# One written order for the stages of all units, with u and g loaded as rows and the weight casts spread over three engines

## The chip, the cores and the metric

The kernel runs on 1 core of one Trainium2 chip. The metric is the device time of one execution in microseconds, the lower the better; one launch of the kernel does the whole computation once.

## What is computed

Two layers follow each other. The first is a linear attention with a decaying state (4 batches, 8 heads, 768 steps, head size 48):

```
for t in range(S):
    cur = einsum('bhd,bhe->bhde', u * k[t], v[t])
    y[t] = einsum('bhd,bhde->bhe', r[t], state + cur)
    state = w[t][..., None] * state + einsum('bhd,bhe->bhde', k[t], v[t])
```

Its output, as 3072 tokens of 384 numbers, goes through a layer of 1024 hidden units whose activation is `h * softmax(h)`, then normalised and scaled by g:

```
h = x @ w_in
solu = h * softmax(h)
ln = (solu - mean(solu)) / sqrt(var(solu) + 1e-6) * g_ln
out = ln @ w_out
```

## The kernel before

The 768 steps are cut into 6 chunks of 128, and a unit is one chunk of one batch: 24 units, batch running fastest, so that units 0 to 3 are the first chunks of the four batches and have no state yet, and units 20 to 23 are the last ones and leave none. For each unit four inputs (w, k, r, v) of 128 x 384 float32 are loaded in 192-byte pieces. The stages of a unit, with the names used below and in the change:

- `lw` (ACT): logarithm of w. `cum` (PE): its running sums forward, two matmuls into one PSUM tile. `exp` (ACT): their exponentials in place. `kp`, `rp` (DVE): k and r times these.
- `vb`, `p`, `q` (POOL): v in bf16; r times k; that times u. `dg` (DVE): the sum of q per head. `dv` (POOL): v times that sum, the term of the present step.
- `krk`, `krr` (PE): transposes of kp and rp; `kr` (DVE): their copy to SBUF. `M` (PE): scores; `m` (ACT): their copy; `sel` (POOL): the causal mask on them, in place. `Y` (PE): attend, which sums the dv term, the state's part and the masked scores times v; `y` (ACT): its copy.
- `S` (PE), `et` (ACT), `st` (DVE): the new state of the batch.
- `X` (PE), `xT` (DVE): transposes of y. `H` (PE): 24 hidden matmuls; `e` (ACT): exp; `he` (DVE): h times e. `Oa`, `Ob` (PE): the output matmuls in two halves, with the sums that the normalisation needs; `junk` (DVE), `sq` (ACT), `qm` (POOL), `lv` (ACT): the scale of each token; `o` (ACT): the scaled output, then the store.

Once per run the weights are prepared: w_in is cast to bf16 (`setup_w_in`), and w_out is multiplied by g (`gw`, eight slices), its column mean is subtracted by PE (`mean`) and the result written to `w2` (`setup_w_out`). `InOrder` makes each engine issue its instructions in the order in which the program is written, and an engine waits at the first instruction whose inputs are missing. That order is made by a loop over ticks (the end of the function): in each tick every stage is called for one unit, at a fixed distance from the tick's number, `setup_w_in` in tick 1 and `setup_w_out` in tick 3. The loads stand in SP's queue: unit 0, u (as a broadcast to 128 partitions), w_in, unit 1, w_out, g, unit 2, and so on. PSUM holds 2 buffers of two banks (tag b: cum, m and h) and 4 of one bank (tag s: all others); loads have 5 buffers each and work tiles 3.

Of the kernel before, what the change touches and what calls it, by code (L numbers as in the profile page):

```python
# [41 lines left out]
def kernel(  # L42
# [76 lines left out]
    win_f = consts.tile([128, KM, DF], F32)  # L119
    nc.sync.dma_start(out=win_f, in_=moe_w_in.rearrange("(ko ki) f -> ki ko f", ki=128))  # L120
    load(1)
    wout_f = consts.tile([128, KF, DM], F32)
    nc.sync.dma_start(out=wout_f, in_=moe_w_out.rearrange("(ko ki) d -> ki ko d", ki=128))
    g_sb = consts.tile([128, KF], F32)
    nc.sync.dma_start(out=g_sb, in_=moe_g_ln.rearrange("(ko ki) -> ki ko", ki=128))
    load(2)
# [7 lines left out]
    def setup_w_in():
        for j in range(KM):
            dve.tensor_copy(out=win_sb[:, j, :], in_=win_f[:, j, :])

    def setup_w_out():

        gr = consts.tile([128, KF], F32)  # L140
        dve.tensor_scalar(out=gr, in0=g_sb, scalar1=RDF, scalar2=None, op0=MULT)
        gw = consts.tile([128, KF, DM], BF16)
        for f in range(KF):
# [12 lines left out]
    def cumulate(i):
        L = live[i]
        lw = L["lw"]
        cum = big.tile([C, 2, 512], F32, tag="b", name="cum_ps")
# [5 lines left out]
        cum = live[i]["ex"]  # L165
        act.activation(out=cum[:, :, :DM], in_=cum[:, :, :DM], func=EXP)

    def scaled(i):
# [1 line left out]
        kp, rp = kp_t[i % NR], rp_t[i % NR]  # L170
        ex = L["ex"][:, :, :DM].rearrange("t e (h d) -> t e h d", h=H)
        dve.tensor_mul(out=kp[:, :, :D], in0=ex[:, 0], in1=L["k"])
        dve.tensor_mul(out=rp[:, :, :D], in0=ex[:, 1], in1=L["r"])
        L["kp"], L["rp"] = kp, rp

    def bonus(i):
# [1 line left out]
        vb = wk.tile([C, H, D], BF16, tag="vb", name="vb")
        pool.tensor_copy(out=vb, in_=L["v"])
        p = wk.tile([C, H, D], BF16, tag="p", name="p")  # L180
        pool.tensor_mul(out=p, in0=L["r"], in1=L["k"])
        q = wk.tile([C, H, D], BF16, tag="q", name="q")
        pool.tensor_mul(out=q, in0=p, in1=u_bc)
        dg = wk.tile([C, H], F32, tag="dg", name="dg")
        L["q"], L["dg"], L["vb"] = q, dg, vb
# [4 lines left out]

    def bonus_v(i):
# [3 lines left out]
        pool.tensor_mul(out=dv, in0=vb, in1=dg.unsqueeze(2).to_broadcast([C, H, D]))  # L195
        L["dv"] = dv

    def transposed(i):
# [1 line left out]
        kr_ps = small.tile([C, 2 * HP, C], BF16, tag="s", name="kr_ps")  # L200
        for j, t in ((0, L["kp"]), (1, L["rp"])):
            for hp in range(HP):
                pe.transpose(kr_ps[:, j * HP + hp, :], t[:, 2 * hp:2 * hp + 2, :].rearrange("t a d -> t (a d)"), ident)
        L["kr_ps"] = kr_ps
# [168 lines left out]
    def store(i):  # L373
        L = live[i]
        c, b = units[i]
        o = io.tile([C, DM], F32, tag="o", name="o")
# [1 line left out]
        nc.sync.dma_start(out=out[b * S + c * C:b * S + (c + 1) * C, :], in_=o)

    LOOK = 4  # L380
    for t in range(-2, NU + 4):
        def do(d, *stages):
            if 0 <= t + d < NU:
                for stage in stages:
                    stage(t + d)

        if t > -2 and t + LOOK < NU:
            load(t + LOOK)
        if t == 1:
            setup_w_in()  # L390
        if t == 3:
            setup_w_out()
        do(0, bonus_v, transposed, transposed_copy)
        do(-1, state, state_decay)
        do(-2, hidden_mul)
        do(-1, state_update)
        do(-3, lambda i: output(i, 0))
        do(-4, store)
        do(-1, x_transposed, x_copy)
        do(1, log_w, bonus)  # L400
        do(0, scores, scores_copy, scores_mask)
        do(1, cumulate, decays)
        do(-3, lambda i: output(i, 1), squares, sums, centre, scale)
        do(1, scaled, bonus_sum)
        do(-1, hidden, hidden_exp)
        do(0, attend, y_copy)


# [28 lines left out]
```

## Time and profile before

| what | value |
|---|---|
| median of 3 runs | 186.49 us (185.88 to 186.62) |
| the profiled execution | 187.83 us |
| its span, first to last instruction | 186.1 us |
| mean granted TensorE clock | 0.952 |
| PE busy | 151.1 us (81%) |
| DVE, ACT, POOL busy | 120.1, 113.4, 108.0 us |
| DMA | 27.28 MB, mean 147 GB/s |

Busy shares are averages over the span. The span has a start, in which loads and weights arrive, and a long regular part; the views below are taken by stretch.

### The profile page before, as it was taken

The page shows a single profiled execution, that of the slowest core. Times are in us where ns is not written, and L with a number is a line of the kernel's source. Part 1 is how long each engine was busy: PE and PEld are TensorE (multiplying, and loading weights), DVE is VectorE, ACT ScalarE, POOL GpSimd, SP SyncE. Part 2 cuts the span into 40 slices and gives each one's busy share as a digit, 9 for nine tenths or more (in the row PEclk, how much of TensorE's full clock was granted, in tenths as well). Part 3 has the DMA queues.
Part 4 walks back from the last instruction along what each step waited for, and adds up shares of the span by engine and source line. Part 5 has one row for each costly group of instructions (what it writes and reads, how often), then busy time and mean ns, then how long its engine had stood idle before and what let it go on. Part 6 is the DMA issues. An engine that isn't in the chain of part 4 may idle for free.

```text
span 186.1 us, 5430 instructions
## 1 busy us (share of the span) xinstructions
PE 151.1 (81%) x2136; PEld 117.1 (63%) x2136; DVE 120.1 (65%) x262; ACT 113.4 (61%) x237; POOL 108.0 (58%) x154
## 2 busy tenths in 40 slices
PE   0312483865999999999999999999999999999980
PEld 0100362533578778787788778787788777787750
...
PEclk9999999585589999999999999999999999999999
...
GB/s 117 260 255 246 221 196 188 166 178 201 188 33 186 138 170 158 202 164 140 196 189 220 179 218 155 166 175 170 153 154 81 48 48 17 29 42 46 42 42 86
DMA packets 105945, 27.28 MB, mean 147 GB/s; under 512 B 101312, under 2 KB 105536, under 8 KB 105920
## 3 DMA queue, kind: packets, MB, share of 16 engines
...
HBM read 22.22 MB, written 4.72 MB: 145 GB/s over the span
## 4 chain that ended last, share of the span: by engine, by line
PE 33%; ACT 29%; POOL 13%; issue 13%; DVE 6%; DMA 3%; SPq 1%; POOLq 0%; DVEq 0%
PE o_ps L34 13%; ACT m L34 9%; ACT e L34 9%; POOL m L34 7%; PE g_ps L34 5%; ACT y L34 4%; PE m_ps L34 4%; PE h_ps L34 4%; DMA u_bc<-in_u_dram 3%; ACT lv L34 3%; PE x_ps L34 2%; DVE gw L34 2%; ACT rs L34 2%; POOL qm L34 2%; DVE w L34 2%
## 5 line engine op out<-in xcount | busy, mean ns | idle before, releaser
L34 PE MATMUL o_ps<-w,he 128*128 128x385 bf16 x192 | 53.9, 331 | 4.7 <-DVE w L34 2.2
L34 PE MATMUL g_ps<-he 128*128 128x128 bf16 x192 | 42.5, 222 | 1.1 <-ACT y L34 1.1
L34 POOL TENSOR_SCALAR_AFFINE_SELECT m<-m 128x1024 bf16<-128x1024 bf16 x24 | 26.2, 1092 | 22.5 <-ACT m L34 22.5
L34 PE MATMUL h_ps<-xT,win_sb 128*128 128x128 bf16 x576 | 38.7, 227 | 0.4 <-ACT m L34 0.2
L34 ACT CAST m<-m_ps 128x1024 bf16<-128x1024 f32 x24 | 24.3, 1011 | 20.4 <-PE m_ps L34 20.4
L34 PEld LDWEIGHTS <-win_sb 128*128 128x128 bf16 x576 | 35.0, 102 | 1.7 <-DVE xT L34 1.1
L34 PEld LDWEIGHTS <-he 128*128 128x128 bf16 x384 | 26.8, 98 | 9.8 <-issue 4.3
L34 POOL TENSOR_TENSOR dv<-vb,dg 128x384 bf16<-128x384 bf16 x24 | 20.3, 847 | 21.8 <-DVE dg L34 20.2
L34 PE MATMUL o_ps<-inv_col,e 128*128 128x1 bf16 x192 | 32.2, 168 | 0.0
L34 DVE TENSOR_TENSOR he<-h_ps,e 128x1024 bf16<-128x1024 f32 x24 | 29.2, 1215 | 4.6 <-ACT e L34 4.6
L34 PEld LDWEIGHTS <-e 128*128 128x128 bf16 x192 | 18.9, 98 | 16.5 <-issue 3.2
L34 ACT ACTIVATE e<-h_ps 128x1024 bf16<-128x1024 f32 x24 | 24.2, 1009 | 4.7 <-PE h_ps L34 4.7
L34 DVE COPY kr<-kr_ps 128x1024 bf16<-128x1024 bf16 x24 | 16.6, 690 | 11.8 <-PE kr_ps L34 11.8
L34 POOL TENSOR_TENSOR p<-r_in,k_in 128x384 bf16<-128x384 f32 x24 | 24.1, 1004 | 0.0
L34 POOL TENSOR_TENSOR q<-p,u_bc 128x384 bf16<-128x384 bf16 x24 | 22.0, 917 | 3.1 <-DMA u_bc<-in_u_dram 1.3
L34 DVE SCALAR_TENSOR_TENSOR junk<-g_ps,ident 128x128 bf16<-128x128 f32 x24 | 7.0, 291 | 22.3 <-PE o_ps L34 22.3
L34 ACT ACTIVATE cum_ps<-cum_ps 128x768 f32<-128x768 f32 x24 | 19.3, 804 | 1.3 <-PE cum_ps L34 1.3
L34 DVE TENSOR_REDUCE dg<-q 128x8 f32<-128x384 bf16 x24 | 13.0, 543 | 8.8 <-POOL q L34 8.8
L34 DVE TENSOR_TENSOR kp<-cum_ps,k_in 128x384 bf16<-128x384 f32 x23 | 12.8, 557 | 8.0 <-ACT cum_ps L34 6.8
L34 POOL CAST vb<-v_in 128x384 bf16<-128x384 f32 x23 | 11.7, 510 | 10.8 <-DMA v_in<-in_v_dram 10.8
L34 ACT ACTIVATE lw<-w_in 128x384 bf16<-128x384 f32 x23 | 11.9, 518 | 9.2 <-DMA w_in<-in_w_dram 9.2
L34 PEld LDWEIGHTS <-kr 64*128 64x128 bf16 (+1 forms) x272 | 11.5, 99 | 8.6 <-DVE kr L34 5.1
...
## 6 DMA issues: line engine op xcount, KB each, us to landing
...
```

The lines of the kernel that those rows point to most:

```text
L34: made = make(*args, **kwargs)
```

## The change

The tick loop is gone. A string ORDER names every stage of every unit (`M3` is the scores of unit 3), and a loop at the end calls them in that order. Its beginning and its end:

```
lw0 cum0 vb0 p0 win1 rows ubc exp0 q0 kp0 p1 rp0 lw1 cum1 dg0 win2 win0 exp1 kp1 krk1 krk0 rp1 krr0 kr0 gw3 M0 dv0 krr1 q1 kr1 m0 dg1 M1 sel0 m1 gw0
lw2 vb1 dv1 sel1 p2 Y0 vb2 gw1 cum2 Y1 y0 gw4 X0 exp2 gw5 gw2 q2 gw6 gw7 kp2 rp2 y1 xT0 lw3 S1 krk2 krr2 kr2 S0 X1 et1 dg2 cum3 st1 exp3 dv2 xT1 M2
mean m2 mean_sb sel2 kp3 et0 H0 e0 p3 rp3 H1 Y2 lw4 q3 w2 he0 krk3 krr3 y2 Oa0 kr3 st0 e1 M3 vb3 Ob0 X2 m3 cum4 lw5 p4 dg3 exp4 dv3 S2 he1 sel3 junk0
...
e23 Ob21 junk21 sq21 Oa22 he23 qm21 lv21 o21 Ob22 junk22 sq22 qm22 Oa23 lv22 Ob23 o22 sq23 junk23 qm23 lv23 o23
```

The rest of it, cut to what matters:

```diff
-    pe, act, dve, pool = (InOrder(tc, e) for e in (nc.tensor, nc.scalar, nc.vector, nc.gpsimd))
+    pe, act, dve, pool, sp = (InOrder(tc, e) for e in (nc.tensor, nc.scalar, nc.vector, nc.gpsimd, nc.sync))
...
-    io = ctx.enter_context(tc.tile_pool(name="io", bufs=5))
-    wk = ctx.enter_context(tc.tile_pool(name="wk", bufs=3))
+    io = ctx.enter_context(tc.tile_pool(name="io", bufs=6))
+    wk = ctx.enter_context(tc.tile_pool(name="wk", bufs=5))
...
+    u_row = consts.tile([1, DM], F32)
+    sp.dma_start(out=u_row, in_=u.rearrange("(o h) d -> o (h d)", o=1))
+    g_rows = consts.tile([KF, 128], F32)
+    sp.dma_start(out=g_rows, in_=moe_g_ln.rearrange("(ko ki) -> ko ki", ki=128))
     load(0)
+    win_f = consts.tile([128, KM, DF], F32)
+    sp.dma_start(out=win_f, in_=moe_w_in.rearrange("(ko ki) f -> ki ko f", ki=128))
+    load(1)
+    wout_f = consts.tile([128, KF, DM], F32)
+    wout_v = moe_w_out.rearrange("(ko ki) d -> ki ko d", ki=128)
+    for half in range(2):
+        part = slice(half * KF // 2, (half + 1) * KF // 2)
+        sp.dma_start(out=wout_f[:, part, :], in_=wout_v[:, part, :])
+    for i in range(2, 5):
+        load(i)
...
-    NR = 3
-    lw_t = [consts.tile([C, H, 64], BF16, name=f"lw{j}") for j in range(NR)]
+    NR = 6
+    lw_t = [consts.tile([C, H, 64], BF16, name=f"lw{j}") for j in range(2 * NR)]
...
-    u_bc = consts.tile([C, H, D], F32)
-    nc.sync.dma_start(out=u_bc, in_=u.partition_broadcast(C))
...
+    def setup_rows():
+        u_ps = small.tile([C, DM], F32, tag="s", name="u_ps")
+        pe.matmul(u_ps, lhsT=ones_row, rhs=u_row, start=True, stop=True)
+        g_ps = small.tile([128, KF], F32, tag="s", name="gt_ps")
+        pe.transpose(g_ps, g_rows, ident_f)
+        live[0]["u_ps"], live[0]["g_ps"] = u_ps, g_ps
+
+    def setup_rows_copy():
+        dve.tensor_copy(out=u_bc.rearrange("t h d -> t (h d)"), in_=live[0]["u_ps"])
+        dve.tensor_scalar(out=gr, in0=live[0]["g_ps"], scalar1=RDF, scalar2=None, op0=MULT)
+
+    def setup_w_in(j):
+        copy = (act.copy, dve.tensor_copy, pool.tensor_copy)[j]
+        copy(out=win_sb[:, j, :], in_=win_f[:, j, :])
+
+    def setup_gain(f):
+        if f % 2:
+            act.activation(out=gw[:, f, :], in_=wout_f[:, f, :], func=COPY, scale=gr[:, f:f + 1])
+        else:
             dve.tensor_scalar(out=gw[:, f, :], in0=wout_f[:, f, :], scalar1=gr[:, f:f + 1], scalar2=None, op0=MULT)
...
-        dve.tensor_add(out=w2[:, :, :DM], in0=m_ps.unsqueeze(1).to_broadcast([128, KF, DM]), in1=gw)
+        live[0]["mean_ps"] = m_ps
+
+    def setup_mean_copy():
+        act.copy(out=mean_sb, in_=live[0]["mean_ps"])
+
+    def setup_w2():
+        for f in range(KF):
+            dve.tensor_add(out=w2[:, f, :DM], in0=gw[:, f, :], in1=mean_sb)
...
+        L["vb"] = wk.tile([C, H, D], BF16, tag="vb", name="vb", bufs=8)
...
+    loaded = 5
+    for word in ORDER.split():
+        if word in once:
+            once[word]()
+            continue
+        name = word.rstrip("0123456789")
+        i = int(word[len(name):])
+        if name == "lw":
+            while loaded < min(i + 5, NU):
+                load(loaded)
+                loaded += 1
+        stages[name](i)
```

u is now bf16 in SBUF. The stages themselves are as before, but for `scaled`, `bonus` and `transposed`, which are cut into single steps that ORDER can place apart, with the same instructions.

Where the instructions move, first on POOL, the start of the program. Before, from unit 0's v cast on (the mask is AFFINE_SELECT, q is p times u_bc):

```order
12 L31 CAST vb<-v_in 128x384
13 masks.py:199 AFFINE_SELECT ident<-ident 128x128
14 L34 TENSOR_TENSOR p<-r_in,k_in 128x384
15 L34 TENSOR_TENSOR q<-p,u_bc 128x384
16 L34 TENSOR_TENSOR dv<-vb,dg 128x384
17 L34 CAST vb<-v_in 128x384
18 L34 TENSOR_TENSOR p<-r_in,k_in 128x384
19 L34 TENSOR_TENSOR q<-p,u_bc 128x384
20 L34 AFFINE_SELECT m<-m 128x1024
21 L34 TENSOR_TENSOR dv<-vb,dg 128x384
22 L34 CAST vb<-v_in 128x384
```

And now, from the q of unit 0 on:

```order
17 L63 TENSOR_TENSOR q<-p,u_bc 128x384
18 L63 TENSOR_TENSOR p<-r_in,k_in 128x384
19 L63 CAST win_sb<-win_f 128x1024
20 L63 TENSOR_TENSOR dv<-vb,dg 128x384
21 L63 TENSOR_TENSOR q<-p,u_bc 128x384
22 L63 AFFINE_SELECT m<-m 128x1024
23 L63 CAST vb<-v_in 128x384
24 L63 TENSOR_TENSOR dv<-vb,dg 128x384
25 L63 AFFINE_SELECT m<-m 128x1024
26 L63 TENSOR_TENSOR p<-r_in,k_in 128x384
27 L63 CAST vb<-v_in 128x384
```

Before, the mask of unit 0 (row 20) stood behind unit 1's cast of v, and the mask of unit 1 behind unit 2's (row 22). Now the masks of both stand ahead of unit 2's first product (row 26), and the mask of unit 0 ahead of unit 1's cast; a cast of w_in has come to POOL.

On DVE, the preparation of the weights. Before, from the casts of w_in to the first `he` behind the output weights:

```order
25 L34 CAST win_sb<-win_f 128x1024 x3
...
39 L34 TENSOR_SCALAR gr<-g_sb 128x8
40 L34 TENSOR_SCALAR gw<-wout_f,gr 128x384 x8
41 L34 TENSOR_TENSOR w_145<-mean_ps,gw 128x8x384
42 L34 COPY kr<-kr_ps 128x1024
43 L34 TENSOR_TENSOR he<-h_ps,e 128x1024
```

And now, from DVE's first instruction that waits for a load:

```order
34 L60 CAST win_sb<-win_f 128x1024
35 L63 CAST u_bc<-u_ps 128x384
36 L63 TENSOR_SCALAR gr<-gt_ps 128x8
37 L63 TENSOR_TENSOR kp_147<-cum_ps,k_in 128x8x48
...
44 L63 TENSOR_SCALAR gw<-wout_f,gr 128x384 x4
45 L63 TENSOR_TENSOR kp_149<-cum_ps,k_in 128x8x48
...
53 L63 TENSOR_TENSOR rp_156<-cum_ps,r_in 128x8x48
54 L63 TENSOR_TENSOR w_192<-gw,mean_sb 128x384 x8
55 L63 TENSOR_TENSOR he<-h_ps,e 128x1024
```

One cast of w_in now stands ahead of unit 0's kp (row 37). Four of the gw (the other four are ACT's) stand ahead of unit 2's kp (row 45), where all eight stood behind unit 3's; the eight adds that make w follow unit 3's rp (row 53).

## Rows read from the trace of the kernel before

**Rows 1.** The page's slices of the span: PE's busy tenths and granted clock.

```profile
PE   0312483865999999999999999999999999999980
...
PEclk9999999585589999999999999999999999999999
```

**Rows 2.** Windows: busy us (count) by engine, granted clock, DMA share, GB/s.

```profile
31.30:38.60 7.30, 6.50 (x70) 5.06 (x71) 5.40 (x11) 3.46 (x6) 5.23 (x7) 0.54 1.09 172
38.60:46.50 7.90, 4.04 (x25) 2.05 (x23) 7.33 (x9) 1.39 (x4) 2.32 (x3) 0.72 1.05 191
46.50:55.00 8.50, 8.09 (x86) 5.79 (x87) 4.98 (x12) 3.83 (x9) 2.55 (x5) 0.66 0.88 122
...
91.00:151.00 60.00, 58.94 (x912) 46.98 (x911) 45.91 (x102) 46.38 (x101) 44.17 (x61) 1.00 0.76 156
```

**Rows 3.** PE's timeline, the start: start us, us, instruction, idle time before it.

```profile
20.78 0.50 PE L34 MATMUL y_ps<-vb,m 128*128 128x48 bf16 x8 [4.86 <-POOL m L34]
...
25.47 2.72 PE L34 MATMUL h_ps<-xT,win_sb 128*128 128x128 bf16 x24 [0.24 <-ACT m L34]
...
31.31 0.37 PE L34 MATMUL y_ps<-vb,m 128*128 128x48 bf16 x8 [2.80 <-POOL m L34]
```

**Rows 4.** POOL's timeline, the start.

```profile
17.23 0.50 POOL L34 CAST vb<-v_in 128x384 bf16<-128x384 f32 x1 [4.98 <-DMA v_in<-in_v_dram]
...
20.69 1.26 POOL L34 TENSOR_TENSOR dv<-vb,dg 128x384 bf16<-128x384 bf16 x1
27.76 0.50 POOL L34 CAST vb<-v_in 128x384 bf16<-128x384 f32 x1 [5.81 <-DMA v_in<-in_v_dram]
```

**Rows 5.** DVE's timeline, the start: the weights.

```profile
20.18 2.92 DVE L34 CAST win_sb<-win_f 128x1024 bf16<-128x1024 f32 x3
...
37.56 4.97 DVE L34 TENSOR_SCALAR gw<-wout_f,gr 128x384 bf16<-128x384 f32 x8
43.10 3.36 DVE L34 TENSOR_TENSOR w<-mean_ps,gw 128x3072 bf16<-128x3072 f32 x1 [0.57 <-PE mean_ps L34]
```

**Rows 6.** PE's timeline, one steady unit.

```profile
90.84 0.32 PE L34 MATMUL o_ps<-w,he 128*128 128x385 bf16 x1
...
92.16 0.40 PE L34 MATMUL m_ps<-kr 64*128 64x128 bf16 x8
...
92.82 0.33 PE L34 MATMUL o_ps<-w,he 128*128 128x385 bf16 x1
...
93.81 1.50 PE L34 MATMUL h_ps<-xT,win_sb 128*128 128x128 bf16 x24
95.14 0.33 PE L34 MATMUL y_ps<-dv,ident 128*128 128x384 bf16 x1
...
95.68 0.38 PE L34 MATMUL kr_ps<-ident,kp 128*128 128x128 bf16 x4
...
96.12 0.33 PE L34 MATMUL s_ps<-st,ident 128*128 128x384 bf16 x1
...
96.83 0.32 PE L34 MATMUL o_ps<-w,he 128*128 128x385 bf16 x1
```

**Rows 7.** The page's groups: line, engine, instruction, count; busy us, mean ns.

```profile
L34 POOL TENSOR_SCALAR_AFFINE_SELECT m<-m 128x1024 bf16<-128x1024 bf16 x24 | 26.2, 1092 | 22.5 <-ACT m L34 22.5
...
L34 ACT CAST m<-m_ps 128x1024 bf16<-128x1024 f32 x24 | 24.3, 1011 | 20.4 <-PE m_ps L34 20.4
...
L34 POOL TENSOR_TENSOR dv<-vb,dg 128x384 bf16<-128x384 bf16 x24 | 20.3, 847 | 21.8 <-DVE dg L34 20.2
...
L34 DVE TENSOR_TENSOR he<-h_ps,e 128x1024 bf16<-128x1024 f32 x24 | 29.2, 1215 | 4.6 <-ACT e L34 4.6
...
L34 DVE COPY kr<-kr_ps 128x1024 bf16<-128x1024 bf16 x24 | 16.6, 690 | 11.8 <-PE kr_ps L34 11.8
...
L34 DVE TENSOR_TENSOR kp<-cum_ps,k_in 128x384 bf16<-128x384 f32 x23 | 12.8, 557 | 8.0 <-ACT cum_ps L34 6.8
```

**Rows 8.** PE's timeline, its last matmul.

```profile
180.92 0.17 PE L34 MATMUL o_ps<-inv_col,e 128*128 128x1 bf16 x1
```

More of the change, by code (lines that the diff above doesn't have):

```diff
@@ new lines @@
+dg5 sel4 qm1 H3 krr5 Oa2 kr5 lw7 e3 lv1 q6 cum6 Y4 vb6 he3 exp6 dv5 y4 p7 q7 o1 kp6 Ob2 M5 X4 rp6 junk2 m5 krk6 sq2 qm2 cum7 lw8 krr6 S3 xT4 kr6 exp7
+H4 sel5 dg6 et3 Oa3 p8 q8 vb7 lv2 st3 Y5 e4 kp7 o2 y5 rp7 Ob3 M6 S4 he4 dv6 sq3 X5 cum8 junk3 m6 S5 et4 xT5 qm3 sel6 st4 lv3 krk7 et5 H5 krr7 exp8 o3
+p9 Y6 st5 q9 Oa4 kp8 y6 lw10 e5 krk8 kr7 X6 rp8 krr8 xT6 M7 kr8 vb9 Ob4 m7 he5 sq4 dg7 sel7 lw9 S6 dv7 vb8 dg9 junk4 M8 m8 p10 qm4 H6 et6 cum9 st6 e6
+Y7 y7 exp9 Oa5 X7 dg8 Ob5 he6 xT7 kp9 q10 junk5 lv4 sel8 o4 rp9 dv8 lw11 sq5 H7 krk9 qm5 krr9 e7 kr9 lv5 dv9 Oa6 he7 o5 p11 M9 m9 Ob6 cum10 junk6 sel9
@@ new lines @@
+Y8 cum11 p12 dg10 Y9 exp10 kp10 sq6 y8 qm6 y9 X8 lv6 exp11 rp10 krk10 krr10 xT8 o6 kr10 kp11 S9 S7 vb11 rp11 et9 et7 H8 lw12 Oa7 st7 p13 M10 q13 Ob7
+st9 X9 e8 vb12 krk11 he8 m10 vb10 lw13 cum12 xT9 krr11 q11 sq7 S8 dg11 et8 dv10 kr11 H9 sel10 p14 vb13 junk7 st8 lw14 exp12 Oa8 Y10 e9 Ob8 qm7 lv7
+kp12 y10 krk12 q14 rp12 dv11 M11 o7 he9 junk8 sq8 dg13 X10 m11 cum13 q12 qm8 S10 xT10 dg12 et10 krr12 p15 exp13 st10 sel11 H10 lv8 Oa9 p16 kr12 o8 e10
+kp13 vb15 Y11 dv13 Ob9 rp13 lw16 krk13 y11 dv12 lw17 vb16 M12 he10 sq9 X11 junk9 m12 qm9 krr13 xT11 S11 et11 H11 kr13 Oa10 lw15 lv9 st11 q16 sel12 q15
@@ new lines @@
+dg16 e11 dg14 o9 Y12 he11 dg15 y12 M13 Ob10 cum14 m13 junk10 exp14 X12 xT12 S12 H12 vb14 kp14 rp14 krk14 et12 krr14 p17 kr14 sel13 Y13 sq10 e12 st12
+y13 he12 M14 m14 qm10 Oa11 dv15 X13 cum15 Ob11 sel14 dv14 exp15 xT13 H13 lv10 vb19 kp15 lw19 junk11 rp15 p18 o10 krk15 krr15 Y14 S13 e13 q17 sq11 kr15
+y14 qm11 et13 M15 he13 st13 Oa12 m15 cum16 lv11 vb17 exp16 cum17 X14 Ob12 xT14 o11 sq12 sel15 S14 kp16 junk12 rp16 qm12 et14 exp17 krk16 dv16 Y15
+krr16 H14 p19 q19 y15 p20 st14 lw18 kr16 lv12 X15 kp17 Oa13 e14 rp17 vb20 M16 xT15 he14 Ob13 vb18 krk17 junk13 q18 cum18 o12 m16 S15 exp18 krr17 sq13
@@ new lines @@
+sel16 et15 qm13 dg17 kr17 lv13 H15 st15 Oa14 e15 Y16 kp18 Ob14 p21 y16 o13 dv17 rp18 sq14 X16 he15 lw23 xT16 dg18 M17 krk18 H16 junk14 qm14 krr18 m17
+sel17 Oa15 e16 kr18 q20 Y17 lw20 lv14 he16 vb21 M18 y17 Ob15 dg19 junk15 m18 cum19 X17 xT17 S17 exp19 kp19 sq15 H17 o14 lw22 e17 sel18 dv18 krk19 et17
+rp19 krr19 kr19 dv19 Y18 qm15 M19 S18 y18 m19 X18 he17 et18 xT18 st18 lw21 cum20 exp20 H18 st17 Oa16 sel19 Y19 kp20 q21 p22 e18 y19 Ob16 rp20 krk20
+lv15 sq16 o15 krr20 he18 junk16 cum21 kr20 X19 qm16 xT19 exp21 S16 et16 st16 dg20 M20 Oa17 dv20 m20 lv16 kp21 S19 o16 Ob17 krk21 rp21 et19 H19 st19
@@ L20 @@
+"""
 class InOrder:
@@ L110 @@
     for j in range(NR):
-        for t in (lw_t[j], kp_t[j], rp_t[j]):
+        for t in (lw_t[j], lw_t[NR + j], kp_t[j], rp_t[j]):
             nc.vector.memset(t[:, :, D:], 0.0)
@@ L115 @@
         nc.vector.memset(st_t[b], 0.0)
-    u_bc = consts.tile([C, H, D], F32)
-    nc.sync.dma_start(out=u_bc, in_=u.partition_broadcast(C))
[L119 to L126, printed above, removed]
     win_sb = consts.tile([128, KM, DF], BF16)
@@ L132, with setup_mean @@
     nc.vector.memset(w2[:, :, DM:], 1.0 / RDF)
[L134 to L143, printed above, removed]
+    ident_f = consts.tile([KF, KF], F32)
+    make_identity(nc, ident_f)
+    ones_row = consts.tile([1, C], F32)
+    nc.vector.memset(ones_row, 1.0)
+    u_bc = consts.tile([C, H, D], BF16)
+    gr = consts.tile([128, KF], F32)
+    gw = consts.tile([128, KF, DM], BF16)
+    mean_sb = consts.tile([128, DM], BF16)
+    def setup_rows():
[14 more added lines that the diff above has]
+        else:
             dve.tensor_scalar(out=gw[:, f, :], in0=wout_f[:, f, :], scalar1=gr[:, f:f + 1], scalar2=None, op0=MULT)
+    def setup_mean():
         m_ps = small.tile([128, DM], F32, tag="s", name="mean_ps")
@@ L166, in decays, with scaled_k, scaled_r, bonus_rk @@
         act.activation(out=cum[:, :, :DM], in_=cum[:, :, :DM], func=EXP)
-    def scaled(i):
+    def scaled_k(i):
         L = live[i]
[L170 to L176, printed above, removed]
-        L = live[i]
[L178 to L185, printed above, removed]
+        L["kp"] = kp_t[i % NR]
+        ex = L["ex"][:, 0, :DM].rearrange("t (h d) -> t h d", h=H)
+        dve.tensor_mul(out=L["kp"][:, :, :D], in0=ex, in1=L["k"])
+    def scaled_r(i):
+        L = live[i]
+        L["rp"] = rp_t[i % NR]
+        ex = L["ex"][:, 1, :DM].rearrange("t (h d) -> t h d", h=H)
+        dve.tensor_mul(out=L["rp"][:, :, :D], in0=ex, in1=L["r"])
+    def bonus_rk(i):
+        L = live[i]
+        L["p"] = wk.tile([C, H, D], BF16, tag="p", name="p")
+        pool.tensor_mul(out=L["p"], in0=L["r"], in1=L["k"])
+    def bonus_u(i):
+        L = live[i]
+        L["q"] = wk.tile([C, H, D], BF16, tag="q", name="q")
+        pool.tensor_mul(out=L["q"], in0=L["p"], in1=u_bc)
+    def v_cast(i):
+        L = live[i]
+        L["vb"] = wk.tile([C, H, D], BF16, tag="vb", name="vb", bufs=8)
+        pool.tensor_copy(out=L["vb"], in_=L["v"])
     def bonus_sum(i):
         L = live[i]
+        L["dg"] = wk.tile([C, H], F32, tag="dg", name="dg")
         dve.reduce_sum(out=L["dg"], in_=L["q"], axis=AX)
@@ L196, in bonus_v, with transposed @@
         L["dv"] = dv
-    def transposed(i):
+    def transposed(i, j):
         L = live[i]
[L200 to L204, printed above, removed]
+        if j == 0:
+            L["kr_ps"] = small.tile([C, 2 * HP, C], BF16, tag="s", name="kr_ps")
+        t = L["rp"] if j else L["kp"]
+        for hp in range(HP):
+            pe.transpose(L["kr_ps"][:, j * HP + hp, :], t[:, 2 * hp:2 * hp + 2, :].rearrange("t a d -> t (a d)"), ident)
     def transposed_copy(i):
@@ L377, in store, with part @@
         act.activation(out=o, in_=L["o_ps"][:, :DM], func=COPY, scale=L["rs"])
[L378 to L406, printed above, removed]
+        sp.dma_start(out=out[b * S + c * C:b * S + (c + 1) * C, :], in_=o)
+    def part(stage, j):
+        return lambda i: stage(i, j)
+    stages = dict(
+        lw=log_w, cum=cumulate, exp=decays, kp=scaled_k, rp=scaled_r, p=bonus_rk, q=bonus_u, vb=v_cast, dg=bonus_sum,
+        dv=bonus_v, krk=part(transposed, 0), krr=part(transposed, 1), kr=transposed_copy, M=scores, m=scores_copy,
+        sel=scores_mask, Y=attend, y=y_copy, X=x_transposed, xT=x_copy, S=state, et=state_decay, st=state_update,
+        H=hidden, e=hidden_exp, he=hidden_mul, Oa=part(output, 0), Ob=part(output, 1), junk=squares, sq=sums, qm=centre,
+        lv=scale, o=store, win=setup_w_in, gw=setup_gain,
+    )
+    once = dict(rows=setup_rows, ubc=setup_rows_copy, mean=setup_mean, mean_sb=setup_mean_copy, w2=setup_w2)
+    loaded = 5
[10 more added lines that the diff above has]
+        stages[name](i)
 _INS = ['r', 'k', 'v', 'w', 'u', 'moe_w_in', 'moe_w_out', 'moe_g_ln']
```

9 lines of the change are left out of this document (7 added, 2 removed).

## The prediction

> **What bounds the kernel now.** I read the slices of the page first, to see where TensorE (PE) is not full. PE's digits stay at 0 to 8 for ten of the forty slices, read 9 for most of the rest, and in slices 8 to 12 PEclk is about half [rows 1]. So there are two kernels in one: a start of some 55 us in which PE waits and, when it runs, runs at 1.2 GHz; and a steady part in which PE is the bound. The windows give the sizes: from 91 to 151 us PE is busy 58.94 of 60 us, while from 38.6 to 46.5 it is busy 4.04 of 7.9 us with the sixteen DMA engines full [rows 2].
>
> Why PE waits in the start is read from PE's own timeline. It waits 4.86 us and then 2.80 us for POOL's mask of the scores (m) before the two first attend stages [rows 3]. POOL was late because it takes its instructions in order: ahead of the mask of unit 0 stands the cast of unit 1's v, which sat 4.98 us for its load, until 17.23; ahead of the mask of unit 1 the cast of unit 2's v, which sat 5.81 us, until 27.76 [rows 4]. So work whose data were there waited behind work whose data were not. The third hole is DVE's: the eight gw and the one w of the output weights hold it from 37.56 to 46.46 [rows 5], and PE's first output matmul needs w. Of PE's clock the rows say this: 24 hidden-layer matmuls took 2.72 us at 25.47 [rows 3] against 1.33 in the steady part (93.81 to 95.14) [rows 6]. I go by these durations, since the clock line shows full level at 25 us. From 46.5 to 55 the granted clock averages 0.66 [rows 2]: at levels 0.5 and 1.0 that is 2.7 us at full level, so PE, working without a hole from 46.5 on, had it back at about 52.3, 5.8 us later.
>
> The steady part: one unit takes 5.99 us (90.84 to 96.83). From start to start its pieces are: the output two halves of 0.99 (92.82 to 93.81), hidden 1.33, scores and cumulate 0.66, attend 0.54, the eight transposes 0.44, state taken like these 0.44, and three transposes of y 0.17 (3/24 of hidden) [rows 6]. The sum is 5.56, so 0.43 us per unit is waiting.
>
> **What PE must do in all.** 24 x 5.56 = 133.4. The first four units have no state yet, which takes 768 columns or about 0.33 off each, by the 0.17 for 384 below (1.3); the last four have no state stage (1.8). The mean's eight matmuls of 384 columns add 1.3, at 0.17 each, two thirds of an output triple's 0.25 (0.99/4). Together 131.6 us at full clock. The change removes none of it.
>
> **The change, part by part.**
>
> *Order at the start.* POOL's masks of units 0 and 1 now stand ahead of unit 1's v cast and of unit 2's product. Between unit 1's last landing (17.2) and unit 2's (27.8) [rows 4] POOL has the product p, a w_in cast, dv, q, mask, vb, dv, mask: eight instructions of 0.5 to 1.3 us (vb 0.50 [rows 4], dv 0.847, mask 1.092 [rows 7], the cast vb's 0.50 times 1024/384 = 1.3), about 8 us of 10.6. Both masks are done before 27.8, so the waits of 4.86 and 2.80 us lose their cause. In the same stretch DVE has kp and rp of unit 1 (1.1), two kr (1.4) and two sums (no longer than kp) [rows 7], and its four gw at 0.62 (4.97/8) [rows 5]: about 6 us, which fits. What is late next is unit 2 itself: its landing hardly moves, since the order of bytes in the queue is the same (unit 0, w_in, unit 1, w_out, unit 2), with 0.2 MB of spread u (about 1 us at 191 GB/s [rows 2]) less and two tiny loads more. PE still waits before 27.8; it only does more inside that time.
>
> *Where PE becomes full.* After v of unit 2 at 27.8 the longest chain is kp and rp (2 x 0.557), half the transposes (0.44 at half clock), kr (0.690) [rows 7] and 0.4 allowed for handoffs: scores of unit 2 start at 30.5 at the latest. Behind them stand the mean and hidden of units 0 and 1, ready before, so from here PE has no reason to stop. By then it has done four cumulates, three sets of transposes, and scores, attend, y transposes and state of two units: 4.9 us. 126.7 remain.
>
> *DVE's block.* w_out is loaded between units 1 and 2, so gw's inputs are there by 27.8. w now hangs on the mean, ending near 30.5 + 0.7 + 2.6 = 33.8, a copy on ACT (0.4 to 1.0, from the 1024-wide cast at 1.011 [rows 7]), and eight adds. One instruction did that work in 3.36 [rows 5]; no bf16 add lies in the trace, so I bound it by 0 and 3.4 and take 3.4. With he (1.215 [rows 7]) the first output can start at 39.2. PE, from 33.8, has two hidden, an attend and eight transposes, 3.6 us at full clock and 7.3 at half: with the first hidden at half and the rest between, it is busy until 38.7 to 41.1. So the cover holds to within 0.5 us. Without it each us of w is a us of the end.
>
> A POOL dv beside the w_in casts of DVE took 1.26 us [rows 4], 0.41 more than the mean of 0.847 [rows 7]. The Trainium skill (SBUF — State Buffer, Who interferes with whom) says that a DVE instruction with two SBUF inputs shares a port with GpSimd's reads and that the loser blocks for the whole instruction; the eight adds are now such instructions, and POOL's p and q of unit 3 stand beside them. By that rule the output weights would be up to 2 us later (two POOL instructions of about 1 us each) and the sum up to 2 us higher, against 0.4 by the row; the trace agrees in kind, not in that size. The sum goes by the row, whose 0.4 lies within the 0.5 us above.
>
> *u and g as rows.* The trace has no float32 matmul. The 384 columns take 0.34 at half clock by the hidden row (2.72/24 x 3), and even ten times that fits before unit 1's data, when PE has nothing else. I take nothing; if it lasted beyond 17 us all of unit 0 would follow.
>
> *Casts of w_in.* DVE's three took 2.92 [rows 5]. Now one each on DVE, ACT and POOL, 1.0 to 1.9 (DVE's 0.97, POOL's 1.3 plus 0.4 to 0.6 if it is blocked). DVE's stands ahead of u, kp and rp of unit 0, so these wait until w_in has landed, which is before unit 1 (17.2). That delays unit 0 by many us, but it would only wait for unit 1's place in the order anyway. Zero, bounded by 1.
>
> *More buffers, more memsets.* Fifteen small memsets on DVE before any data: nothing. Six instead of five load buffers let loads run further ahead; the stretch is already DMA-full [rows 2].
>
> *Clock.* From 30.5 PE runs without a hole, so I expect 5.8 us at half level as after 46.5: 2.9 us lost, between 0 (if the run began earlier) and 6.
>
> *Waits later.* The new order mixes units differently, hidden of the next unit standing between most exps and outputs. The other engines are at 44 to 46 us in 60 [rows 2], so they neither bind nor leave much room. I take half of today's 0.43 over some 19 units: 4.1, ends 1 and 10.
>
> *End.* From PE's last matmul (180.92) [rows 8] to the end of the span, 186.1, is 5.2 us; the same chain stays.
>
> **Sum:** 30.5 + 126.7 + 2.9 + 4.1 + 5.2 = 169.4 of span. Before, the profiled execution took 187.83 with a span of 186.1, so 171.1; the median of the runs is 186.49, 1.3 under it, so 169.8. I say 169.5.
>
> **Rivals.**
>
> *Late start* (0.17): some head of a queue waits for a load that lands later than I think (DVE's w_in cast, an ACT gw ahead of unit 0's copy, POOL's p of unit 2), so PE has new holes around 30 us, and the clock stays at half for longer. For it: before, the granted clock averaged 0.54 to 0.72 from 31.3 to 55 through such holes [rows 2]. Against: the list has ready work behind most of these heads. Five us of start and three of clock: 175 to 180.
>
> *Loads bind* (0.08): then the order gains less than it says. After 27.8 a unit's 0.786 MB at 172 to 191 GB/s [rows 2] takes 4.1 to 4.6 us, a store of 0.197 MB 1.0 to 1.1. With 21 units and some 16 stores the last load lands at 130 to 143; behind it stand about 24 us of PE work and the 5.2: 160 to 172 of span, or up to 173. It stays under the PE sum or just reaches it.
>
> *PSUM stalls* (0.08, slower): all of cum, m and h share two big buffers. A unit holds them for 0.33 + 0.76 + 2 x 0.557 (cum; its exp is three quarters of the cast's 1.011), 0.33 + 1.011 (m) and 1.33 + 1.0 + 1.215 (h; its exp taken as the cast) [rows 6, 7]: 7.1, with handoffs some 8 us, or 4 of 5.56 on two buffers. A regular order spaces them; an irregular one, as where two cumulates stand in a row, makes hidden wait for rp. Without waits the time would be 165.7; to reach 186.5 it takes 20.8 us, about 1.0 per unit, over twice today's 0.43. From there on the change is slower: 187 to 192. DVE's slack speaks against it.
>
> *Almost no waits and an earlier full clock* (0.05): 161 to 164.
>
> **How the numbers follow.** My forecast, 164 to 175, has 0.60; late start 0.17; loads 0.08; stalls 0.08; better 0.05; the rest, 0.02, is no change. A measurement of this kernel can tell about 0.5% from nothing, 0.9 us; all but the last two kinds lie far below. Faster 0.90, same 0.02, slower 0.08. The range for 8 in 10 takes the forecast, the loads and most of the late start: 163.5 to 178.5.
>
> **What would show it.** Right: POOL's masks of units 0 and 1 before 27 us; PE gapless from about 30; half clock gone by 37; first output near 40; ticks of 5.6 to 5.9. Wrong: PE holes over 1 us after 31, a wait of the first output for w, hidden waiting on rp, or loads waited for after 40 us.

## The result and the profile after

The changed kernel takes 171.8 us (median of 4, 171.34 to 172.43) against 186.19 us for the kernel before on the same chip: a ratio of 0.924 (95% interval 0.919 to 0.929). The profiled execution took 171.34 us with a span of 169.6. The forecast of 169.5 was 1.4% low; range and sign held.

The slices of the page, in the form of [rows 1]:

```profile
PE   0503669939899999999999999999999999999980
...
PEclk9999999987999999999999999999999999999996
```

A slice is 4.24 us here. PE is full from the seventh slice, 25 us, where it took ten slices and 46.5 us before; one large hole is left in the ninth (a 3, 34 to 38 us) and a small one in the eleventh (8). Before PE's last matmul PEclk dips only in the ninth and tenth (8, 7), where it fell to 5 before; the 6 at the end stands behind that matmul. The windows of the changed kernel (columns as in [rows 2]):

```profile
30.00:37.00 7.00, 4.37 (x70) 3.83 (x68) 5.76 (x10) 3.46 (x7) 4.61 (x5) 1.00 1.11 180
37.00:46.00 9.00, 8.06 (x98) 5.94 (x99) 7.17 (x16) 5.22 (x12) 4.98 (x7) 0.81 1.31 178
46.00:55.00 9.00, 9.00 (x146) 7.43 (x144) 7.30 (x15) 7.40 (x14) 8.61 (x13) 1.00 1.13 194
55.00:91.00 36.00, 35.96 (x578) 29.61 (x576) 30.24 (x68) 30.07 (x67) 30.77 (x43) 1.00 1.05 199
91.00:151.00 60.00, 59.43 (x949) 48.54 (x946) 46.13 (x102) 47.53 (x100) 41.03 (x58) 1.00 0.60 124
```

In 91 to 151 PE runs 949 matmul instructions where it ran 912 [rows 2], so a unit takes 5.99 x 912/949 = 5.76 us. From 46 us on PE has next to no hole (59.43 of the 60 us at 91 to 151). The start of PE's timeline, against [rows 3]:

```profile
22.11 0.50 PE L63 MATMUL y_ps<-vb,m 128*128 128x48 bf16 x8 [0.69 <-POOL m L63]
...
24.76 0.50 PE L63 MATMUL y_ps<-vb,m 128*128 128x48 bf16 x8 [0.69 <-POOL m L63]
...
28.18 0.61 PE L63 MATMUL m_ps<-kr 64*128 64x128 bf16 x8
28.72 2.15 PE L63 MATMUL mean_ps<-gw,mean_w 128*128 128x384 bf16 x8
30.71 2.84 PE L63 MATMUL h_ps<-xT,win_sb 128*128 128x128 bf16 x48
...
33.98 0.39 PE L63 MATMUL kr_ps<-ident,rp 128*128 128x128 bf16 x4
37.30 0.50 PE L63 MATMUL o_ps<-w,he 128*128 128x385 bf16 x1 [2.94 <-DVE he L63]
```

The two waits for the mask are 0.69 each instead of 4.86 and 2.80. Unit 2's scores start at 28.18, and 48 hidden matmuls in 2.84 us are at full clock (24 took 2.72 before [rows 3]). Then PE stops for 2.94 us, and from 37.3 to about 40.2 it is at the lower of its two levels, 1.2 GHz: a 385-column matmul takes 0.50, later 0.32. What it waits for is on DVE, and beside it stands POOL (two timelines, the same stretch; the second fence is POOL's):

```profile
31.42 4.69 DVE L63 TENSOR_TENSOR w<-gw,mean_sb 128x384 bf16<-128x384 bf16 x8 [1.24 <-ACT mean_sb L63]
36.03 1.21 DVE L63 TENSOR_TENSOR he<-h_ps,e 128x1024 bf16<-128x1024 f32 x1
```

```profile
31.19 1.00 POOL L63 TENSOR_TENSOR p<-r_in,k_in 128x384 bf16<-128x384 f32 x1
32.27 0.91 POOL L63 TENSOR_TENSOR q<-p,u_bc 128x384 bf16<-128x384 bf16 x1
33.13 0.63 POOL L63 CAST vb<-v_in 128x384 bf16<-128x384 f32 x1
33.72 1.10 POOL L63 TENSOR_TENSOR p<-r_in,k_in 128x384 bf16<-128x384 f32 x1
```

The eight adds of w take 4.69 us, not the 3.4 of the forecast, and the first output waits for `he` behind them. PE's last matmul stands at 164.64, 5.0 us before the end of the span (5.2 before [rows 8]):

```profile
164.64 0.17 PE L63 MATMUL o_ps<-inv_col,e 128*128 128x1 bf16 x1
```

### The profile page after: what moved, and what is told of

Read it like the earlier page. It is cut to its first block, busy times and chain, and to the rows that moved or that the text cites. A ratio compares the mean times of both kernels' runs of the same rounds, so it can differ in the third digit from the quotient of the medians.

```text
span 169.6 us, 5377 instructions
## 1 busy us (share of the span) xinstructions
PE 144.7 (85%) x2139; PEld 114.4 (67%) x2139; DVE 119.8 (71%) x280; ACT 118.2 (70%) x243; POOL 107.4 (63%) x157
## 4 chain that ended last, share of the span: by engine, by line
PE 78%; DVE 6%; DMA 5%; ACT 3%; SPq 2%; POOL 2%; issue 2%; POOLq 0%; DVEq 0%
PE o_ps L63 22%; PE h_ps L63 18%; PE kr_ps L63 7%; PE g_ps L63 6%; PE y_ps L63 6%; PE m_ps L63 5%; PE s_ps L63 5%; DMA w_in<-in_w_dram 5%; PE cum_ps L63 4%; PE x_ps L63 3%; DVE w L63 3%; SPq L63 2%; POOL m L63 1%; DVE kr L63 1%; PE mean_ps L63 1%
## 5 line engine op out<-in xcount | busy, mean ns | idle before, releaser
L63 PE MATMUL o_ps<-w,he 128*128 128x385 bf16 x192 | 51.8, 330 | 2.9 <-DVE he L63 2.9
L63 PE MATMUL h_ps<-xT,win_sb 128*128 128x128 bf16 x576 | 35.9, 219 | 0.0
L63 PEld LDWEIGHTS <-win_sb 128*128 128x128 bf16 x576 | 32.8, 98 | 0.8 <-DVE xT L63 0.5
L63 PEld LDWEIGHTS <-he 128*128 128x128 bf16 x384 | 24.5, 97 | 4.9 <-DVE he L63 3.1
L63 POOL TENSOR_TENSOR dv<-vb,dg 128x384 bf16<-128x384 bf16 x24 | 19.8, 828 | 10.1 <-DVE dg L63 10.0
L63 DVE TENSOR_TENSOR kp<-cum_ps,k_in 128x384 bf16<-128x384 f32 x24 | 13.4, 556 | 4.8 <-ACT cum_ps L63 4.0
L63 PEld LDWEIGHTS <-kr 64*128 64x128 bf16 (+1 forms) x272 | 11.5, 99 | 6.3 <-DVE kr L63 2.8
L63 POOL TENSOR_TENSOR qm<-ss,sq 128x1 f32<-128x1 f32 x24 | 4.5, 189 | 17.2 <-DVE junk L63 13.7
L63 DVE TENSOR_TENSOR st<-s_ps,et 64x192 bf16<-64x192 f32 x40 | 14.1, 352 | 1.6 <-ACT et L63 0.6
L63 ACT ACTIVATE o<-o_ps,rs 128x384 f32<-128x384 f32 x24 | 13.9, 579 | 0.3
```

The source lines that it names most:

```text
L63: made = make(*args, **kwargs)
```

## The experiments

Each was timed in three rounds, the last in five, with the kernel before on the same chip (its median 186.1 to 186.4). Intervals are of the ratio to it, at 95%.

**What the order is worth.** Three kernels keep the change's rows, casts and buffers and write the string anew.

*tick_all*: the words in the tick order of before, all through.

```diff
-lw0 cum0 vb0 p0 win1 rows ubc exp0 q0 kp0 p1 rp0 lw1 cum1 dg0 win2
...
+lw0 rows ubc vb0 p0 q0 cum0 exp0 kp0 rp0 dg0 dv0 krk0 krr0 kr0 lw1 vb1 p1 q1 M0 m0 sel0
...
```

> The changed kernel with its own parts (u and g as rows, weight casts on three engines, more buffers) but with the order of the old tick loop, weights in ticks 1 and 3 as before. Theory A, the written order at the start brings most of the gain and the parts little: 181 to 186 us; POOL again waits for v of units 1 and 2 ahead of the masks, PE is not full before 40. Theory B, the parts and buffers bring most: 172 to 177.

Measured: 181.62 us, ratio 0.977 (0.972 to 0.982). So all parts other than the order (rows, shared casts, buffers, the order of the loads) give 4.5 us together; the time lies in theory A's range, and the rest of the gain is the order's. The waits for the mask are back at 4.57 and 2.08, and from 91 to 151 PE has 908 matmuls, about as before (912). But the adds of w, which here run with POOL idle, take 2.24 us:

```profile
40.61 2.24 DVE L63 TENSOR_TENSOR w<-gw,mean_sb 128x384 bf16<-128x384 bf16 x8 [2.00 <-ACT mean_sb L63]
```

*start_then_tick*: the string as changed up to `junk1`, then the tick order. *tick_then_order*: ticks -2 to 3, then the words of the changed string that are still to come.

> The written order up to the scale of unit 1 (four lines of it, to about 46 us), then the old tick order for all that is left. Theory A: the steady part goes back to about 6.0 us a unit, some 0.24 more on 19 units, so about 4.6 more than the change: 175 to 178. Theory C, the steady order brings as much as the start or more (all of the 0.43 of waits per unit): 180 or more.

> The old tick order through tick 3 (w_out included), then the written order for what is left. Theory A: the start's holes are back, only the steady gain stays: 180 to 183. Theory C: 177 or less.

Measured: 178.43 us, 0.962 (0.954 to 0.969), and 179.03 us, 0.963 (0.958 to 0.968). From 181.62, the start's order alone gives 3.2 us, the rest alone 2.6, both together 9.8: they are not additive. Both times lie just outside theory A's ranges (0.4 over, 1.0 under) and clear of theory C's. The windows 91 to 151, of start_then_tick and then of tick_then_order, show the pace going with the rest of the order:

```profile
91.00:151.00 60.00, 58.63 (x912) 46.86 (x910) 45.46 (x100) 46.12 (x100) 44.29 (x62) 1.00 0.66 135
```

```profile
46.00:55.00 9.00, 6.65 (x83) 5.05 (x82) 4.19 (x10) 5.11 (x11) 4.83 (x7) 0.88 1.07 185
91.00:151.00 60.00, 59.44 (x947) 48.72 (x945) 48.13 (x106) 48.84 (x103) 43.03 (x61) 1.00 0.62 130
```

912 against 947 matmuls is 0.22 us a unit, some 4.2 over 19 units. What hides it in tick_then_order is the seam between the two orders: PE is busy 6.65 of the 9 us at 46 to 55. In start_then_tick the tick order also holds at the end, where PE is busy 12.88 of the 14 us at 151 to 165, against 13.81 in the change. So neither half alone has a clean price.

*mask_first*: the kernel before, with POOL's mask ahead of the next unit's vb, p and q in every tick; nothing else.

```diff
-        do(1, log_w, bonus)
+        do(1, log_w)
         do(0, scores, scores_copy, scores_mask)
+        do(1, bonus)
```

> The kernel before with one thing moved: in each tick POOL's mask of unit t stands ahead of vb, p and q of unit t+1. Theory A: the waits of 4.86 and 2.80 us of PE for the mask shrink to under 1, but DVE's block of gw and w from about 37 to 46 still holds the first output, so only 2 to 4 us are won: 182 to 185. If the mask were the whole cause of the late start: 176 to 180. If the loads alone set the start: 186, no change.

Measured: 233.7 us, ratio 1.259 (1.251 to 1.268); every time that was expected is missed, though the waits for the first two masks did shrink (0.95 us for unit 0's, none for unit 1's). POOL's timeline from one steady mask to the next, then ACT's and PE's:

```profile
89.63 1.09 POOL L34 TENSOR_SCALAR_AFFINE_SELECT m<-m 128x1024 bf16<-128x1024 bf16 x1 [3.56 <-ACT m L34]
90.67 0.50 POOL L34 CAST vb<-v_in 128x384 bf16<-128x384 f32 x1
91.13 1.00 POOL L34 TENSOR_TENSOR p<-r_in,k_in 128x384 bf16<-128x384 f32 x1
92.21 0.92 POOL L34 TENSOR_TENSOR q<-p,u_bc 128x384 bf16<-128x384 bf16 x1
93.09 0.19 POOL L34 TENSOR_TENSOR qm<-ss,sq 128x1 f32<-128x1 f32 x1
93.80 0.83 POOL L34 TENSOR_TENSOR dv<-vb,dg 128x384 bf16<-128x384 bf16 x1 [0.52 <-DVE dg L34]
97.94 1.09 POOL L34 TENSOR_SCALAR_AFFINE_SELECT m<-m 128x1024 bf16<-128x1024 bf16 x1 [3.31 <-ACT m L34]
```

```profile
93.31 0.29 ACT L34 ACTIVATE lv<-sq,qm 128x1 f32<-128x1 f32 x1 [2.02 <-POOL qm L34]
...
93.75 1.01 ACT L34 ACTIVATE e<-h_ps 128x1024 bf16<-128x1024 f32 x1
94.65 0.47 ACT L34 CAST y<-y_ps 128x384 bf16<-128x384 f32 x1
```

```profile
95.17 0.32 PE L34 MATMUL o_ps<-w,he 128*128 128x385 bf16 x1 [1.24 <-ACT y L34]
...
96.41 0.40 PE L34 MATMUL m_ps<-kr 64*128 64x128 bf16 x8
```

The mask now waits for its scores with the next unit's products queued behind it: 84.2 us in 23 waits. Behind the products stands `qm`. ACT takes its instructions in order too: its `lv` waits for `qm` (54.5 us in 24 waits, 14.1 in the kernel before), `e` and `y` stand behind `lv`, PE's output matmuls wait for `y`, and the next scores stand behind them. So mask, products, `qm`, `lv`, `e`, `y`, output and next scores make one ring of 8.3 us a unit (97.94 - 89.63); `dv` lies beside it, since it ends 3.31 us before the next mask. The move that the first two units need is ruinous as a rule; it takes an order that differs from unit to unit.

**The hole before the first output.** In the next three `w2` stands for the adds of w.

*w2_pool_held*: POOL's p, q of unit 3 come after w2 in the string, and p begins with a copy that needs w2.

```diff
+        if i == 3:
+            hold = wk.tile([C, 1], BF16, tag="hold", name="hold")
+            pool.tensor_copy(out=hold, in_=w2[:, KF - 1, DM - 1:DM])
```

*w2_psum*: w in one instruction that reads the mean from PSUM, the form of before [rows 5], so that ACT's copy of the mean goes too; POOL unchanged.

```diff
-        for f in range(KF):
-            dve.tensor_add(out=w2[:, f, :DM], in0=gw[:, f, :], in1=mean_sb)
+        dve.tensor_add(out=w2[:, :, :DM], in0=live[0]["mean_ps"].unsqueeze(1).to_broadcast([128, KF, DM]), in1=gw)
```

*w2_halves*: four adds, then unit 0's `he`, then the other four.

> The changed kernel with POOL kept out of the way of w: a one-element copy that reads w's last slice stands ahead of p and q of unit 3 (these moved behind w), so POOL rests while DVE makes the eight adds. Theory P, the adds are blocked by POOL's instructions: the eight take 2.2 to 2.9 us instead of 4.7, he of unit 0 ends some 2 us earlier, PE's hole before the first output is under 1 us and the clock stays up; 168.5 to 170.5, less what the later p and q cost (up to 1). Theory Q, the adds are slow by themselves: still 4.7 and 172 or more.

> w made by one DVE instruction that reads the mean from PSUM, as before the change; POOL's order is untouched and the copy of the mean on ACT is gone. Theory P: with one SBUF input DVE isn't blocked, so 3.4 us beside the same POOL work, first output 1.5 us earlier: 169.5 to 171. Theory Q: 3.4 us too. If it is stretched beside POOL to 4 or more, P falls.

> Only order: the first four adds of w, then he of unit 0, then the other four adds, since the first half of the output needs only four. Both theories: he about 1 us earlier, hole of PE 2 instead of 3 us, second half of the output may wait; 170 to 171.5.

Measured: 170.28 us, 0.912 (0.905 to 0.919); 169.71 us, 0.911 (0.905 to 0.917); 170.06 us, 0.911 (0.904 to 0.919). DVE's timeline in w2_pool_held, in w2_psum and in w2_halves:

```profile
32.09 2.24 DVE L63 TENSOR_TENSOR w<-gw,mean_sb 128x384 bf16<-128x384 bf16 x8 [1.04 <-ACT mean_sb L63]
```

```profile
30.06 3.36 DVE L63 TENSOR_TENSOR w<-mean_ps,gw 128x3072 bf16<-128x3072 f32 x1
```

```profile
29.26 3.54 DVE L63 TENSOR_TENSOR w<-gw,mean_sb 128x384 bf16<-128x384 bf16 x4
32.72 1.21 DVE L63 TENSOR_TENSOR he<-h_ps,e 128x1024 bf16<-128x1024 f32 x1
33.85 1.15 DVE L63 TENSOR_TENSOR w<-gw,mean_sb 128x384 bf16<-128x384 bf16 x4
```

The same eight adds take 2.24 us with POOL held and 4.69 beside it; four take 3.54 beside POOL and 1.15 without. With one operand in PSUM the instruction takes 3.36 beside the same POOL work, which takes no longer either (p 1.00, q 0.91). In w2_psum w also starts 1.36 us earlier than in the change (30.06 against 31.42), without ACT's copy of the mean and with the mean at full clock. PE's hole shrinks from 2.94 to 0.49, 1.02 and 1.49, and the granted clock stays at 1.00 from 30 to 55 in w2_psum. All three are 1.5 to 2.1 us faster than the change by their medians (the upper ends of their intervals, 0.917 to 0.919, lie about at the lower end of its own, 0.919), yet one and the same hidden stage, at 54.01 us in the change, starts at 50.05 to 50.91: about half of the gain was given back later.

*w2_few_loads* and *w2_late* ask where. The first leaves v of units 9 to 23 unloaded and uses unit 8's in its place.

```diff
+            if name == "v" and i > 8:
+                live[i][name] = v_keep
+                continue
```

The second moves `lw`, `vb` and `p` of units 12 to 23 back in w2_psum's string; `ld19` issues the loads where `lw19` did. Around one of them (parts of lines):

```diff
-sel14 dv14 exp15 xT13 H13 lv10 vb19 kp15 lw19 junk11 rp15
+sel14 dv14 exp15 xT13 H13 lv10 kp15 ld19 junk11 rp15
...
+qm14 p20 krr18 m17 sel17 Oa15 e16 kr18 q20 Y17 lw19
```

> w2_psum, with v of units 9 to 23 not loaded: unit 8's v takes its place, so 15 of the 96 loads are left out (2.9 MB); the computation is otherwise the same. In w2_psum H begins some 3.5 us earlier than in the change, but the end comes only 2.1 earlier, and between 86 and 95 us three waits for loads appear (lw on ScalarE 2.86, p and vb on GpSimd 1.73 and 0.83) that the change did not have. Theory L (with the start mended, TensorE overtakes the loads, which the queues bring at some 195 GB/s): without these loads no engine waits for one after 50 us, TensorE is busy for 11.7 or more of 91 to 103 (10.47 in w2_psum), and the time is 167.5 to 168.7. Rival O (the loss there comes from the order of the stages): busy stays at 10.5 to 11 and the time at 169.4 to 170.

> w2_psum, with the first stages of units 12 to 23 that read a load (lw, vb, p) moved back in the order, to six to ten words before the stage that uses their result; the loads are issued where they were. Theory L: the waits for loads at 86 to 105 us no longer hold up what is queued behind them on ScalarE and GpSimd, TensorE is busy for 11.5 or more of 91 to 103, and the time is 168 to 169. Rival O (the moved stages now come just before their users, and TensorE waits for them instead): new waits for POOL or ACT after 91 us and 169.5 to 171.5.

Measured: 168.12 us, 0.902 (0.897 to 0.907), and 168.11 us, 0.903 (0.900 to 0.906). Two rows of the waits of w2_psum, 85 to 110 us (us in total, times, longest):

```profile
ACT lw L63 <- DMA w_in<-in_w_dram: 2.9, 1, 2.9
...
POOL p L63 <- DMA r_in<-in_r_dram: 1.7, 1, 1.7
```

ACT's `lw` waits until 91.73; `lv` and `rs` stand behind it, and at 94.21 PE waits 1.16 us for `rs`.

The windows of w2_psum, w2_few_loads and w2_late:

```profile
91.00:103.00 12.00, 10.47 (x160) 8.28 (x158) 7.88 (x17) 9.09 (x18) 9.01 (x14) 1.00 0.99 197
```

```profile
91.00:103.00 12.00, 11.72 (x192) 9.63 (x190) 8.67 (x19) 9.41 (x18) 8.14 (x11) 1.00 0.48 94
```

```profile
91.00:103.00 12.00, 11.10 (x180) 9.05 (x178) 8.87 (x19) 8.75 (x16) 8.67 (x12) 1.00 1.01 199
```

So the loads took it back: with 15 loads less, PE's loss there is gone (11.72, as the change's 11.73 in the same window; one wait of 0.6 us for a load is left after 50 us); with the readers of the loads moved later, about half of it (0.9 us of 12 left: 0.63 behind POOL's mask, 0.26 behind DVE's kr). w2_late falls short of the 11.5 that was expected. Its interval lies wholly under the change's (0.919 to 0.929): it beats both kernels. Over w2_psum its gain is less sure. The intervals touch, and in the profiled executions 1.2 of the 1.9 us between the two spans are there already at the first output (33.44 against 34.61), ahead of every stage that was moved.

*w2_late_halves*: w2_late with the one addition cut in two around `he0`.

> w2_late, with the single addition into w cut in two: w's first four blocks, then unit 0's he, then the last four. In w2_late TensorE waits 1.27 us for he at 33.44, and the loads still hold GpSimd's p once for 2.6 us. If the start still sets the end, he is ready some 1.7 us earlier, the hole goes (under 0.4 us) and the time is 166.5 to 167.5 against w2_late's 168.11. Rival: the loads take it back, as they took back half of w2_psum's gain; the hole goes, but new waits behind loads come up after 85 us and the time stays at 167.8 to 168.6.

Measured: 169.7 us (167.72 to 171.45), 0.907 (0.902 to 0.913): no gain over w2_late. The hole did not go, it moved one matmul on:

```profile
32.74 0.34 PE L64 MATMUL o_ps<-w,he 128*128 128x385 bf16 x1 [0.23 <-DVE he L64]
34.40 0.22 PE L64 MATMUL g_ps<-he 128*128 128x128 bf16 x1 [1.32 <-DVE w L64]
```

The matmul into g_ps waits for the second addition, though it reads no part of w. The program's order says why: the tiles of tag s take four buffers in turn, and from the mean on they are the mean, y, the transposes, o_ps and then g_ps, which so gets the mean's buffer. With the mean read from PSUM, that buffer is free only when the second addition has read it, at 34.35. No run gives the mean a buffer of its own. Why this kernel's times spread wider is open.

**The other two parts.** *u_broadcast*: u loaded as 128 copies and g as columns, as before; the rest as changed.

```diff
-    sp.dma_start(out=u_row, in_=u.rearrange("(o h) d -> o (h d)", o=1))
+    sp.dma_start(out=u_bc, in_=u.partition_broadcast(C))
```

> u and g loaded as before the change (u spread to 128 partitions by the load in float32, g as columns), right behind unit 0; all else as changed. If the rows matter: w_in and units 1 and 2 land 1 to 2 us later and everything behind shifts: 173 to 174. If they don't: 171.8.

Measured: 173.11 us, 0.929 (0.923 to 0.935), against the change's 171.8. PE's cumulate of unit 1, which waits for that unit's load by way of `lw` (the change's row is in the second fence), and the start of the mean, 30.21 against 28.72, are 1.4 to 1.5 us later:

```profile
15.28 0.48 PE L63 MATMUL cum_ps<-lw,uti_neg 128*128 128x384 bf16 x1 [10.32 <-ACT lw L63]
```

```profile
13.91 0.48 PE L63 MATMUL cum_ps<-lw,uti_neg 128*128 128x384 bf16 x1 [5.14 <-ACT lw L63]
```

The ratios' intervals overlap, so the 1.3 us rest on the traces more than on the times. They belong to u and g together, which this run puts back at once.

*casts_dve*: all eleven weight casts on DVE.

```diff
-        copy = (act.copy, dve.tensor_copy, pool.tensor_copy)[j]
-        copy(out=win_sb[:, j, :], in_=win_f[:, j, :])
+        dve.tensor_copy(out=win_sb[:, j, :], in_=win_f[:, j, :])
...
-        if f % 2:
-            act.activation(out=gw[:, f, :], in_=wout_f[:, f, :], func=COPY, scale=gr[:, f:f + 1])
```

> The change, with all weight casts on VectorE (three of w_in, eight of the gain) as before; order, rows and buffers are the change's. VectorE gets two casts of w_in (0.69 each) and four of the gain (0.41 to 0.77 each) more, some 3.5 us between 12 and 27 us, where it waits some 4 us in all in the changed kernel. Theory A (sharing the casts is worth something): part of it falls on kr, kp2 and the last gain, the mean starts at 29.5 to 31 instead of 28.72, and the time is 172.5 to 174. Rival B (VectorE's waits take all of it): the mean within 0.5 us of 28.72 and 171.3 to 172.3.

Measured: 174.58 us, but over 171.63 to 175.06, and no ratio can be given. The execution of 171.63 is the profiled one, a time as rival B has it. But in it the mean starts at 30.49, as theory A has it, and PE waits longer than in the change, yet it is not slowed behind the wait (PE's timeline):

```profile
30.49 1.48 PE L63 MATMUL mean_ps<-gw,mean_w 128*128 128x384 bf16 x8
...
38.91 0.34 PE L63 MATMUL o_ps<-w,he 128*128 128x385 bf16 x1 [3.37 <-DVE he L63]
```

Its first output is 1.6 us later than the change's (38.91 against 37.30), its span only 0.3 us longer: behind the wait the change ran at 1.2 GHz for 2.9 us, which cost it half of that, and this execution ran at 2.4 GHz. The other three, at 174.4 to 175.1, lie above theory A's 172.5 to 174. Their mean granted clock of 0.984 to 0.986, against 0.992, accounts for an estimated 1.2 us of that (0.007 of 171); only the first was profiled, so the rest is open. What the shared casts are worth is thus an estimated 1.6 us at the first output by the traces, and between nothing and 3 us in the time.

## Why the prediction was right

By its own steps, on the profiled execution:

| term | forecast | measured |
|---|---|---|
| scores of unit 2 start | 30.5 | 28.18 |
| cold clock | 2.9 | 2.5 |
| PE holes after it | 0 | 3.5 |
| PE work left and small waits | 126.7 + 4.1 | 130.4 |
| end | 5.2 | 5.0 |
| span | 169.4 | 169.6 |

The cold clock is worked out from the rows: 0.2 for the scores and 0.8 for the mean (2.15 against eight times 0.17), and half of the 2.9 us from 37.3 to 40.2. The holes are 2.94 and one of 0.57 at 43.20. The fourth measured value is the rest: 169.6 less the others. So the sum came out within 0.2 us of the span, and 171.34 was measured for 171.1. That it is so close is luck: 2.3 us won at the start and 3.5 us of holes that the sum had at nothing nearly cancel. The forecast of the median was low by 2.3: 1.3 because I subtracted the distance of one profiled execution to its median, 0.5 because this one lay under its median and not over, and 0.5 from that 0.2 and from rounding 169.8 down to 169.5. That distance was no property of the kernel. Two of the signs named for being wrong came true: a PE hole over 1 us after 31, and a first output that waits for w.

**Right.** The masks: 20.86 and 23.49, both before 27. Work whose data were there stood behind work whose data were not, and moving it took away both waits; tick_all, without the move, has them back. The steady pace: half of 0.43 us of waits per unit is 0.21, and 5.99 - 5.76 = 0.23 were gained; tick_then_order shows that the order alone does it.

**Wrong: w.** The step that failed is "I bound it by 0 and 3.4 and take 3.4", with the cover that "holds to within 0.5 us". The eight adds took 4.69, outside my bounds, and PE, which was done at 34.36, waited 2.94. The row of 3.36 [rows 5] has one operand in PSUM, and I took it for a bound of adds with both in SBUF. Alone each of these takes 0.35 us; beside POOL three of the eight take 0.98, 1.07 and 1.15, one for each of the products p, q and p (1.00, 0.91 and 1.10). The instruction that reads PSUM is not touched by POOL (3.36 beside it, and 3.36 before, where POOL was idle). The difference that POOL makes, 4.69 - 2.24 = 2.45, is six times the 0.4 that I took from a row. And that row was of another kind: there POOL's dv lost time, beside a cast on DVE that has one input. The Trainium skill (SBUF — State Buffer, Who interferes with whom) says that a DVE instruction with two SBUF inputs and GpSimd's reads share a port, and that the loser is blocked for the whole instruction. The trace agrees: its 2.45 us lies near the up to 2 us that the forecast worked out by that rule and set aside.

**Wrong, and it hid the first.** "Its landing hardly moves": unit 2's v cast ran at 25.62, right behind the mask and r times k, against 27.76 after a wait for its load [rows 4]. u_broadcast puts some 1.5 us of that on the 128 copies of u and on g as columns; I had priced the copies at about 1 us of bytes and then not subtracted it. And "From 30.5 PE runs without a hole, so I expect 5.8 us at half level": PE was at full level already at 30.7, and was back at the lower one after the hole of w.

**The rivals.** Late start did not come: 28.18. PSUM stalls did not come: no matmul of H waits for rp in the trace. Loads bind was not true of the change, whose waits after 50 us hold one of 0.4 us for a load, but it is the next bound: once w2_psum had made the start some 3 to 4 us shorter, ACT and POOL waited for loads at 86 to 95 us, and PE behind them.
